# Tokens side by side as weights in the variance's small products, and the factor written to DRAM in single numbers

## Chip, cores and metric

One core of a Trainium2 chip runs the kernel. The metric is the device time of one execution in microseconds (us). Engines are named as in the profile: PE (TensorE's matmuls), PEld (its weight loads), DVE (VectorE), ACT (ScalarE), POOL (GpSimd), SP (SyncE, here the issuer of nearly all DMAs).

## What is computed

Linear attention over 8 batches of 576 tokens with 8 heads of 64 features, then two feed-forward layers. The change lies in the normalisation at the head of the first of these:

```python
rms = np.sqrt(np.mean(x * x, axis=-1, keepdims=True) + 1e-06)
xn = x / rms * rms_g
g = xn @ w_gate
silu = g * (1.0 / (1.0 + np.exp(-g)))
val = xn @ w_val
return (silu * val @ w_out)
```

Here `x` has 4608 tokens of 512 features, and `w_gate` and `w_val` have 1536 columns each. `1 / rms` is one number for each token; it is called the factor below. The second layer takes the maximum of three products and multiplies it by an output matrix.

## The kernel before

The 4608 tokens are worked in nine groups of 512 (`NG`, `N`). Activations lie by feature: a tile has 128 features on its partitions and 512 tokens along its free dimension, and four such tiles make one group's x. The first mixture layer is a loop over groups g and over 12 slices f of the hidden features, `iteration(g, nxt, f)`; each iteration runs 24 products of 128x128 weights with 128x512 tokens (`product_in`, L601 to L603) into two PSUM banks, `pg` and `pv`. Each product is made from three with operands split into a high and a low part. While group g is multiplied, the attention of the group after next and the normalisation of the next one, `nxt`, are worked out in between, at fixed iterations; products of the second mixture's weights (class `Ahead`) are prepared beside them.

The steps that make the factor of group `nxt` are these, for `nxt` from 3 to 8:

- `make_x` squares the attention's output (ACT) and adds the four tiles of squares up (POOL, L518), so that `sacc[nxt]` holds for each of 128 partitions and 512 tokens a partial sum of squares.
- `token_rstd` (at f = 7) sums over the partitions. Four products on L551 take 128 tokens of `sacc` each as weights and a column of ones as the moving operand; each puts one column with 128 sums into `pv`. The trace shows each of these products as two loads and two matmuls, so that a group has eight. `pv` has 128 partitions and 4 columns.
- DVE turns these into the factor by three Newton steps (L552 to L559), in `z`, of 128 partitions by 4 numbers.
- `z` is put on the list `later`. At the start of the next iteration SP writes it to `rstd_dram[nxt]` in DRAM, 512 numbers in the order of the tokens.
- `read_rstd` (at f = 9) reads these 512 numbers back, the same row for all 128 partitions, into `rooms["zb"]`.
- `normalise` (at f = 10, DVE, L583) multiplies the four tiles of x by it, and `split_x` (at f = 11) makes high and low parts, which the first product of the next group reads.

The factor has to lie in DRAM token by token. Groups that are not in `COMPACT` (groups 3 to 8) choose the tokens so that each partition holds neighbours: column t of the product takes tokens t, t + 4, t + 8 and so on, so that partition r ends with tokens 4r to 4r + 3. Groups 0 to 2 don't go by DRAM; groups 1 and 2 take tokens side by side (128t to 128t + 127) and spread the factor by transposes (`spread_rstd`).

Every DMA of SP is issued by the helper `sp` (L143 from group 1 on, L145 ahead of that), in the order in which the program has them. SP takes them one after the other, and a DMA that waits holds up those behind it. The DMAs take turns on eight semaphores, and each waits until the last one on its own semaphore has landed. The statistics of q (`stats_dram`) go through DRAM in the same way as the factor: `put_stat` writes them, `spread_stats` reads them, in four DMAs of which each fills 64 partitions of one of two planes.

Here are SP's rows from the write of group 3's factor on, with what each waits for. `rstd` is the factor's place in DRAM, `stats` that of q's statistics, `rooms_o` rooms for tiles that are used again, `w_dram` the prepared weights, `h_dram` the stored hidden features, `kT` and `q` inputs of the attention.

```order
L143 DMA rstd_194<-z_3_2702 128x4 [waits DMAHW0_49,DVE_49]
L143 DMA h_dram_2_116<-h_7_2742 128x512 [waits DMAHW1_49,DVE_49]
L143 DMA w_dram_146<-rooms_o_1420 128x512 [waits DMAHW2_49,Pool_49]
L143 DMA w_dram_158<-rooms_o_1421 128x512 [waits DMAHW3_49,Pool_49]
L143 DMA w_dram_155<-rooms_o_1420 128x512 [waits DMAHW4_49,Pool_49]
L143 DMA stats_1_172<-qr_1_2689 128x2x4 [waits DMAHW5_49]
L143 DMA rooms_o_1422<-in_qt 128x512 [waits DMAHW6_49]
L143 DMA kT_2_2776<-in_kt 128x576 [waits DMAHW7_49]
L143 DMA q_3_2778<-in_q 128x512 [waits DMAHW0_49,Activation_49]
```

The last of them, q, is the eighth behind the write and waits for the write's own semaphore, `DMAHW0`.

Of the kernel before, what the change touches and what calls it, by code (L numbers as in the profile page):

```python
# [25 lines left out]
COMPACT = (0, 1, 2)  # L26
# [29 lines left out]
def attention_moe_moe(ctx: ExitStack, tc: tile.TileContext, q, qt, k, kt, v, w1, w1_out, rms_g, w2, w2_out, out):  # L56
# [23 lines left out]
    def bank(tag, name):  # L80
        return ps.tile([P, N], F32, tag=tag, name=name)
# [34 lines left out]
    rstd_dram = [dram.tile([N], F32, tag=f"rstd_{g}", name=f"rstd_{g}") for g in range(NG)]  # L116
# [12 lines left out]
    for i in range(2):  # L129
        t = one.tile([P, P], F32, tag=f"kv_raw{i}", name=f"kv_raw{i}")  # L130
# [17 lines left out]
    later, rooms = [], {}  # L148
# [158 lines left out]
    kmax, xraw, sacc, qrt, rstd = {}, {}, {}, {}, {}  # L307
# [229 lines left out]
    def token_rstd(g):  # L537

        var = one.tile([P, LINE], F32, tag="var0", name=f"var0_{g}")[:, 0:4]
        if g == 0:  # L540
            for t in range(4):
                nc.vector.tensor_scalar(
                    var[:, t : t + 1], sacc[0][t][:, 0:1], 1.0 / N, EPS_RMS, op0=ALU.mult, op1=ALU.add
                )
        else:
            pv = bank("a1" if g < BY_FEATURE else "acc2", f"pv_{g}")
            for t in range(4):
                s = sacc[g][:, t * P : (t + 1) * P]
                if g not in COMPACT:
                    s = sacc[g].rearrange("p (r t) -> p t r", t=4)[:, t, :]  # L550
                nc.tensor.matmul(pv[:, t : t + 1], s, ones_f[:, 0:1], start=True, stop=True)  # L551
            nc.vector.tensor_scalar(var, pv[:, 0:4], 1.0 / N, EPS_RMS, op0=ALU.mult, op1=ALU.add)  # L552
        z = one.tile([P, LINE // 2], F32, tag="z0", name=f"z0_{g}")[:, 0:4]
        nc.vector.tensor_scalar(z.bitcast(I32), var.bitcast(I32), -0.5, RSQRT_SEED, op0=ALU.mult, op1=ALU.add)
        a = one.tile([P, LINE // 2], F32, tag="a0", name=f"a0_{g}")[:, 0:4]
        for i in range(3):
            nc.vector.scalar_tensor_tensor(a, z, 0.25**i, z, op0=ALU.mult, op1=ALU.mult)
            nc.vector.tensor_mul(a, a, var)
            nc.vector.scalar_tensor_tensor(z, a, -3.0, z, op0=ALU.add, op1=ALU.mult)  # L559
        rstd[g] = z  # L560
        if g == 0:
            spread_rstd(g)
        if g not in COMPACT:
            later.append((rstd_dram[g].rearrange("(r t) -> r t", t=4), z))

    def read_rstd(g):
        sp(rooms["zb"], rstd_dram[g].unsqueeze(0).to_broadcast([P, N]))
# [2 lines left out]
    def spread_rstd(g):  # L570
        z = rstd[g]
        pr = bank("a1", f"rstd_{g}")
        for t in range(4):
            nc.tensor.transpose(pr[:, t * P : (t + 1) * P], z[:, t : t + 1].to_broadcast([P, P]), ident)
        if g < BY_FEATURE:
            zb = one.tile([P, N], F32, tag="ql", name=f"z_{g}")
        else:
            zb = rooms["zb"]
        nc.scalar.copy(zb, pr)
        rstd[g] = None, zb  # L580
# [43 lines left out]
    for step in range(11):  # L624
        for stage, t in stages:
            if 0 <= step - t < 4:
                stage(0, step - t)
    token_rstd(0)
    for stage in (first.scale, first.join, first.high, first.low):
        for h in range(2):  # L630
# [217 lines left out]
    def iteration(g, nxt, f):  # L848
# [18 lines left out]
        if nxt == 1:  # L867
            if not odd and 1 <= pair <= 4:
                transpose_q(nxt, pair - 1)
                make_kv(nxt, pair - 1)  # L870
                if pair + 1 < 4:
                    load_pair(nxt, pair + 1)
            if odd and 1 <= pair <= 4:
                make_x(nxt, pair - 1)
            if pair < 4 and not odd:
                k_max(nxt, pair)
                q_exp(nxt, pair)
            if pair < 4 and odd:
                k_exp(nxt, pair)
                q_divide(nxt, pair)  # L880
            if f == 10:
                token_rstd(nxt)
            if f == 11:
                for p in range(4):
                    normalise(nxt, p)
# [44 lines left out]
        if nxt is not None and nxt >= BY_FEATURE:  # L930
            if f == at:
                token_rstd(nxt)
            if f == at + 2 and nxt not in COMPACT:
                read_rstd(nxt)
            if f == 10 and nxt > BY_FEATURE:
                for p in range(4):
                    normalise(nxt, p)
# [256 lines left out]
    for pr in range(NPAIR):  # L1194
        behind = []
        for u in range(UNITS):
            fp, j = divmod(u, 3)
            if j == 0:
                t = {
                    key: two.tile([P, N], F32, tag=tag, name=f"t2_{pr}_{fp}_{tag}")  # L1200
                    for key, tag in (((0, 0), "q"), ((0, 1), "k"), ((1, 0), "v"))
                }
# [21 lines left out]
    g = NG - 1  # L1224
# [28 lines left out]
    for u in range(UNITS):  # L1253
        fp, j = divmod(u, 3)
        pair = [bank(tag, f"p2_{g}_{u}_{tag}") for tag in (("G", "V"), ("a0", "a1"))[u % 2]]
        if j == 0:
            t = [two.tile([P, N], F32, tag=tag, name=f"t2_{g}_{fp}_{tag}") for tag in ("q", "k")]
# [83 lines left out]
```

## Time and profile before

| | us |
|---|---|
| median of 3 runs | 1511.15 |
| lowest, highest | 1510.17, 1512.53 |
| the profiled execution, its own time | 1514.36 |
| its span, first to last instruction | 1512.2 |

The profiled execution's time has 2.2 us around its span. The rows further below are from this execution; a time of day in them counts from the span's start. "Idle before" in brackets behind a row is how long the engine stood before it, and behind the arrow stands what ended that.

### The profile page before, as it was taken

How to read it: one execution, taken by the hardware profiler on the slowest of the kernel's cores; microseconds unless marked ns; L12 is line 12 of the kernel's file. 1: busy time of each engine (PE TensorE's matmuls, PEld its weight loads, DVE VectorE, ACT ScalarE, POOL GpSimd, SP SyncE). 2: the span in 40 equal slices, each digit the busy share in tenths (PEclk: the TensorE clock that was granted, in tenths of full speed). 3: DMA queues.
4: the chain of work that ended last, by engine and by line, in shares of the span. 5: the costliest groups of instructions: out<-in, count | busy, mean ns of one | idle time of the engine just before them, and what ended most of it. 6: DMA issues, size and time to landing. Idle time of an engine off the chain costs nothing.

```text
span 1512.2 us, 19762 instructions
## 1 busy us (share of the span) xinstructions
PE 1479.8 (98%) x6692; PEld 1220.0 (81%) x6692; DVE 1059.5 (70%) x1769; ACT 611.0 (40%) x1176; POOL 446.6 (30%) x380
## 2 busy tenths in 40 slices
PE   6899999999999999999999999999999999999999
PEld 4677878788878888888888888888888888888887
DVE  6998786778676765472888989748748748747622
ACT  7754443435343444341545545323423413413311
POOL 0012544444344344351265764111111111111100
PEclk9999999999999999999999999999999999999999
DMA  8866988878887967588545245265585585585572
GB/s 263 307 197 175 258 248 244 268 215 259 245 259 217 265 187 262 195 285 318 177 170 195 82 162 202 79 226 197 194 296 194 194 305 190 189 288 190 181 261 102
DMA packets 159333, 330.30 MB, mean 218 GB/s; under 512 B 31104, under 2 KB 55680, under 8 KB 159232
## 3 DMA queue, kind: packets, MB, share of 16 engines
q1 hardware_dynamic: 155776, 322.74, 65.8%
q10 hardware_dynamic: 3456, 6.29, 1.1%
q8 instruction: 53, 0.87, 0.2%
q14 instruction: 48, 0.39, 0.1%
HBM read 246.42 MB, written 82.55 MB: 218 GB/s over the span
## 4 chain that ended last, share of the span: by engine, by line
PE 70%; DVE 6%; DMA 3%; issue 2%; ACT 1%; SPq 1%; POOL 1%; DVEq 0%; POOLq 0%
PE p_a L608 4%; PE p_a L607 4%; PE p_a L609 4%; PE pg L602 4%; PE pg L601 4%; PE pg L603 4%; PE pv L603 4%; PE pv L602 4%; PE pv L601 4%; PE o_acc L608 3%; PE o_acc L609 3%; PE o_acc L607 3%; PE p_G L607 2%; PE p_G L608 2%; PE p_G L609 2%; PE o_a L607 2%
## 5 line engine op out<-in xcount | busy, mean ns | idle before, releaser
L1067 POOL TENSOR_TENSOR temps_wl<-temps_wl,temps_wh 128x512 f32<-128x512 f32 x36 | 48.2, 1340 | 348.4 <-ACT temps_wh L1066 273.8
L273 POOL TENSOR_TENSOR rooms_o<-st,rooms_o 128x256 fp32r<-128x256 f32 x77 | 65.0, 852 | 126.3 <-ACT rooms_o L272 119.7
L960 DVE SCALAR_TENSOR_TENSOR t<-t,pg 128x512 f32<-128x512 f32 x64 | 43.9, 686 | 69.2 <-ACT t L959 68.5
L1058 DVE TENSOR_TENSOR temps_wl<-temps_wl,p_a 128x512 f32<-128x512 f32 x72 | 49.2, 683 | 37.3 <-POOL temps_wl L1067 37.1
L419 POOL TENSOR_TENSOR q<-q,qm 128x512 f32<-128x512 f32 x29 | 31.8, 1097 | 144.7 <-DVE ks L457 97.7
L1062 ACT COPY temps_wh<-p_G 128x512 f32<-128x512 f32 x36 | 21.1, 587 | 105.9 <-PE p_G L609 105.5
L973 DVE SCALAR_TENSOR_TENSOR h<-t,pv 128x512 f32<-128x512 f32 x66 | 45.2, 685 | 26.3 <-PE pv L603 23.5
L607 PE MATMUL p_a<-x_wh,chunk 128*128 128x512 f32 x160 | 62.2, 389 | 0.0
L608 PE MATMUL p_a<-x_wh,chunk 128*128 128x512 f32 x160 | 62.2, 389 | 0.0
L609 PE MATMUL p_a<-x_wh,chunk 128*128 128x512 f32 x160 | 62.2, 389 | 0.0
L607 PE MATMUL p_a<-x_wl,chunk 128*128 128x512 f32 x160 | 62.2, 389 | 0.0
L608 PE MATMUL p_a<-x_wl,chunk 128*128 128x512 f32 x160 | 62.2, 389 | 0.0
L609 PE MATMUL p_a<-x_wl,chunk 128*128 128x512 f32 x160 | 62.2, 389 | 0.0
L959 ACT ACTIVATE t<-pg 128x512 f32<-128x512 f32 x64 | 37.8, 591 | 51.2 <-PE pg L603 48.8
L1064 DVE TENSOR_TENSOR temps_wl<-temps_wh,p_V 128x512 f32<-128x512 f32 x36 | 24.6, 684 | 43.9 <-PE p_V L609 43.9
L762 POOL TENSOR_TENSOR h_Z<-h_Z,h_X 128x512 f32<-128x512 f32 x24 | 39.8, 1678 | 44.8 <-DVE h_X L755 41.0
L758 POOL TENSOR_TENSOR h_X<-h_Y,h_X 128x512 f32<-128x512 f32 x24 | 40.4, 1694 | 38.9 <-DVE o_xl L101 21.6
L960 DVE SCALAR_TENSOR_TENSOR rooms_o<-rooms_o,pg 128x512 f32<-128x512 f32 x42 | 28.6, 682 | 31.3 <-ACT rooms_o L959 31.1
L272 ACT CAST rooms_o<-st 128x256 fp32r<-128x256 f32 x77 | 31.8, 423 | 39.8 <-DMA w_dram<-rooms_o 16.1
L453 PEld LDWEIGHTS pk<-v,k 128*128 128x128 f32 x300 | 40.5, 204 | 6.4 <-ACT k L444 3.9
L453 PE MATMUL pk<-v,k 128*128 128x129 f32 x300 | 42.2, 290 | 2.9 <-ACT k L444 2.3
L959 ACT ACTIVATE rooms_o<-pg 128x512 f32<-128x512 f32 x42 | 24.9, 593 | 45.3 <-PE pg L603 45.1
(1232 smaller groups left out, 4978.7 us busy)
## 6 DMA issues: line engine op xcount, KB each, us to landing
chunk<-w_dram SPq DMA_DIRECT2D x112, 768.0 KB, 4.3
w_dram<-rooms_o SPq DMA_DIRECT2D x113, 256.0 KB, 3.4
h_dram<-h SPq DMA_DIRECT2D x108, 256.0 KB, 4.4
stat<-stats SPq DMA_DIRECT2D x112, 128.0 KB, 5.3
words<-in_w SPq DMA_DIRECT2D x24, 512.0 KB, 6.6
chunk<-w_dram SPq DMA_DIRECT2D x48, 256.0 KB, 3.6
k<-in_k SPq DMA_DIRECT2D x30, 320.0 KB, 4.6
v<-in_v SPq DMA_DIRECT2D x30, 320.0 KB, 6.1
```

What stands on the lines that cost most here:

```text
L273: nc.gpsimd.tensor_sub(t[:, 1, :], src, t[:, 0, :].bitcast(F32))
L453: nc.tensor.matmul(pk[:, 0 : P + 1], k_t[g, p][:, c, :], v_t[g, p][:, c, :], start=(c == 0), stop=(c == 4))
L601: nc.tensor.matmul(pt, hi[:, j, s], xhs[kk], start=(kk == 0), stop=False)
L602: nc.tensor.matmul(pt, hi[:, j, s], xls[kk], start=False, stop=False)
L603: nc.tensor.matmul(pt, lo[:, j, s], xhs[kk], start=False, stop=(kk == 3))
L607: nc.tensor.matmul(pt, ah, bh, start=first, stop=False, skip_group_check=onto)
L608: nc.tensor.matmul(pt, ah, bl, start=False, stop=False, skip_group_check=onto)
L609: nc.tensor.matmul(pt, al, bh, start=False, stop=last, skip_group_check=onto)
L959: nc.scalar.activation(t, pg, AF.Tanh, scale=0.5)
L960: nc.vector.scalar_tensor_tensor(t, t, 1.0, pg, op0=ALU.add, op1=ALU.mult)
L1058: nc.vector.tensor_add(y, x, pt)
L1067: nc.gpsimd.tensor_add(w, u2, s5)
```

## The change

Two lines of `token_rstd`: the products of all groups take 128 tokens that lie side by side, as groups 1 and 2 do, and column t then holds tokens 128t to 128t + 127. The write to DRAM puts number t of partition r at place 128t + r instead of 4r + t. What lies in DRAM after it, and the read of it, are as before.

```diff
             for t in range(4):
                 s = sacc[g][:, t * P : (t + 1) * P]
-                if g not in COMPACT:
-                    s = sacc[g].rearrange("p (r t) -> p t r", t=4)[:, t, :]
                 nc.tensor.matmul(pv[:, t : t + 1], s, ones_f[:, 0:1], start=True, stop=True)
...
         if g not in COMPACT:
-            later.append((rstd_dram[g].rearrange("(r t) -> r t", t=4), z))
+            later.append((rstd_dram[g].rearrange("(t r) -> r t", t=4), z))
```

No instruction is added, taken away or moved on any engine, and no wait changes. On SP six rows have another form; this is the piece for group 3, with the row ahead of the write and the one behind it:

```order
 L143 DMA stat_0_2679<-stats_0_171 64x512 [waits DMAHW7_49]
-L143 DMA rstd_194<-z_3_2702 128x4 [waits DMAHW0_49,DVE_49]
+L143 DMA rstd_194<-z_3_2702 128x4x1 [waits DMAHW0_49,DVE_49]
 L143 DMA h_dram_2_116<-h_7_2742 128x512 [waits DMAHW1_49,DVE_49]
 L143 DMA w_dram_146<-rooms_o_1420 128x512 [waits DMAHW2_49,Pool_49]
```

The write goes out as 128 x 4 pieces of one number each where it was 128 pieces of four numbers.

## Rows read from the trace of the kernel before

**Rows 1.** Page, part 1: busy us (share of the span) xinstructions.
```profile
PE 1479.8 (98%) x6692; PEld 1220.0 (81%) x6692; DVE 1059.5 (70%) x1769; ACT 611.0 (40%) x1176; POOL 446.6 (30%) x380
```

**Rows 2.** Busy time by stretch: us, PE, PEld, DVE, ACT, POOL, granted clock, DMA share, GB/s.
```profile
195.00:720.00 525.00, 520.34 (x2406) 433.43 (x2405) 340.37 (x653) 213.26 (x420) 218.99 (x211) 1.00 0.81 247
```

**Rows 3.** Weight loads of L551, 195 to 700 and 100 to 195 us: ns min/median/max.
```profile
L551 PEld LDWEIGHTS pv<-ones_f,sacc x48: 308/329/332, 245.9 to 628.6; 128*128 128x128 f32 x48
...
L551 PEld LDWEIGHTS pv<-ones_f,sacc x16: 187/192/192, 107.4 to 182.5; 128*128 128x128 f32 x16
```

**Rows 4.** PE's timeline at group 2's and group 3's burst: start us, us.
```profile
181.80 0.95 PE L551 MATMUL pv<-ones_f,sacc 128*128 128x1 f32 x8
182.61 0.48 PE L601 MATMUL pg<-x,wh_(1, 9)_1184 128*128 128x512 f32 x1
...
245.99 1.92 PE L551 MATMUL pv<-ones_f,sacc 128*128 128x1 f32 x8
247.78 0.47 PE L601 MATMUL pg<-xh,wh_(1, 7)_1041 128*128 128x512 f32 x1
```

**Rows 5.** Chain of waits, the bursts that it holds: start us, us.
```profile
323.25 1.76 PE pv L551 x8
...
477.18 1.76 PE pv L551 x8
...
552.97 1.64 PE pv L551 x8
...
627.38 1.64 PE pv L551 x8
```

**Rows 6.** Chain of waits ahead of group 5's stage, three of its pieces.
```profile
386.74 0.70 DVE h L973
...
403.32 5.11 DMA stat<-stats
...
421.77 5.80 DMA rooms_o<-rstd
```

**Rows 7.** PE's timeline where it stood idle; in brackets the idle time before.
```profile
116.35 0.62 PE L574 MATMUL rstd<-ident,z 128*128 128x128 f32 x4 [2.21 <-DVE z L559]
...
279.87 0.50 PE L601 MATMUL pg<-x,wh_(1, 0)_506 128*128 128x512 f32 x1 [0.18 <-ACT x L100]
281.63 0.50 PE L602 MATMUL pg<-x,wh_(1, 0)_506 128*128 128x512 f32 x1 [1.25 <-DVE x L101]
...
432.58 2.36 PE L453 MATMUL pk<-v,k 128*128 128x129 f32 x10 [1.79 <-ACT k L444]
```

**Rows 8.** Timelines of DVE, SP and POOL behind group 3's burst.
```profile
246.08 0.69 DVE L973 SCALAR_TENSOR_TENSOR h<-t,pv 128x512 f32<-128x512 f32 x1 [0.45 <-PE pv L603]
...
249.33 2.87 SPq L143 DMA_DIRECT2D stat<-stats  x4
...
257.65 1.29 POOL L380 TENSOR_TENSOR qT<-qT,stat 128x512 f32<-128x512 f32 x1 [1.70 <-DMA stat<-stats]
```

**Rows 9.** Busy time by stretch around two idle times; the clock stands third from the end.
```profile
114.00:117.00 3.00, 0.79 (x6) 0.68 (x6) 2.83 (x10) 1.05 (x2) 0.52 (x1) 1.00 0.00 0
...
432.00:437.00 5.00, 4.42 (x17) 3.99 (x18) 5.00 (x10) 2.64 (x5) 1.33 (x1) 0.66 0.95 294
```

**Rows 10.** DMA queue from 631 to 633 us, group 8's write alone: packets, MB, share.
```profile
q1 hardware_dynamic: 144, 0.00, 3.8%
```

**Rows 11.** DMA issues of the whole span, the factor's write: KB, median us to landing.
```profile
rstd<-z SPq DMA_DIRECT2D x6, 2.0 KB, 4.9
```

**Rows 12.** SP's timeline: a load in 640 pieces, then group 4's write and read.
```profile
248.68 0.59 SPq L143 DMA_DIRECT2D v<-in_v  x1
...
335.13 0.38 SPq L143 DMA_DIRECT2D rstd<-z  x1
...
345.98 0.33 SPq L143 DMA_DIRECT2D rooms_o<-rstd  x1
```

**Rows 13.** SP's waits from 485 to 496 us: total us, times, longest.
```profile
SPq L143 <- DMA rstd<-z: 0.6, 1, 0.6
```

## The prediction

> **What bounds the kernel now.** I read the page's busy times first, then the busy time by stretch, then the small products by themselves, the chain of waits, and last what DVE, SP and POOL do where TensorE (PE below) waits. The page gives PE 98% of the span [rows 1]; in the stage of the first mixture, 195 to 720 us, which holds all six places that the change touches, PE is busy for 520.34 of 525 us at the full clock [rows 2]. So an instruction that gets shorter on PE here is worth its time, unless the chain of waits passes that place by on other engines. That exception decides this case.
>
> "The burst of group g" is the run of variance products on L551 for group g: four products, recorded as eight loads and eight matmuls. It stands in the stage of the group before. All groups' loads have the same 128 columns. The 16 of groups 1 and 2, whose weights are tokens side by side, take 192 ns in the median; the 48 of groups 3 to 8, whose weights are every fourth token, take 329 ns [rows 3].
>
> **The change, part by part.**
>
> *The six bursts.* After the change they read what group 2 reads today. From the burst's start to the next product's start, group 2 needs 182.61 - 181.80 = 0.81 us, group 3 needs 247.78 - 245.99 = 1.79 us [rows 4]; both have a transpose right ahead of them. The saving is 0.98 us. The chain gives the bursts of groups 4 and 6 1.76 us each, those of groups 7 and 8 1.64 us each [rows 5]; so I count 0.98 for groups 3 to 6 and 0.98 - 0.12 = 0.86 for groups 7 and 8. Together 4 x 0.98 + 2 x 0.86 = 5.64 us of PE time.
>
> *What of it lies on the path.* The chain runs through four of the bursts, those of groups 4, 6, 7 and 8 [rows 5]. It doesn't run through the other two.
> - Group 5: at 386.74 the chain has left PE for DVE, goes on through SP's issues, a read of the q statistics at 403.32 and the read of the factor at 421.77, and comes back to PE only at 432.58, where PE had stood idle for 1.79 us [rows 6, 7]. The burst at 398 lies beside that. A faster PE only waits longer there: 0.
> - Group 3: the chain as traced starts later than this, so I followed it by hand. The burst starts at 245.99 [rows 4]. DVE makes h at 246.08 from a product that stands ahead of the burst; SP issues four reads of statistics at 249.33; POOL stands idle for 1.70 us for one of them and subtracts at 257.65 [rows 8]. From there it goes by ACT, POOL and SP, with no product behind the burst in it that ends last, to the two idle times of PE at 279.87 and 281.63, 0.18 and 1.25 us [rows 7]. So the 0.98 us turns into idle time there too: 0.
>
> What is left is 2 x 0.98 + 2 x 0.86 = 3.68 us. For groups 3 and 5 the bounds are 0 and the whole 0.98 each; I take 0, since PE already waits there for 1.43 and 1.79 us.
>
> *The factor's write.* Six times, 128 pieces of 16 bytes become 512 pieces of 4 bytes. The trace has no 4-byte piece. The nearest row is the write for group 8, alone on the queues: 144 packets take 3.8% of sixteen engines' 2 us, 0.076 us an engine, or 8.4 ns for each of its nine packets [rows 10]. At that price 384 more pieces, 24 an engine, cost 0.20 us. SP's issue of the write takes 0.38 us; a load of 640 pieces takes 0.59 [rows 12]; so at most 0.2 us more. That is 0.4 us a group.
>
> Its cover: the write lands 4.9 us after issue in the median [rows 11], and the shortest distance from write to read among the six is group 4's, 345.98 - 335.13 = 10.85 us [rows 12], which leaves 5.95 us. But each DMA on SP waits for the one eight places ahead, and in one group, 6, SP stood for 0.6 us waiting for this write [rows 13]. What is queued behind it there are loads of the next pairs and the stores of h. I charge the 0.4 us once, in that group. The bounds are 0 and 6 x 0.4 = 2.4 us.
>
> *The rest.* The order of instructions and their waits is the same on every engine, DVE's work on the factor has the same shape, and the read of the factor stays a read of one row for all partitions: 0.
>
> *Sum.* -3.68 + 0.4 = -3.28, say -3.3 us: 1514.36 - 3.3 = 1511.1 us for the profiled execution. That one stands 3.2 us above the median of the three runs; from the median it is 1511.15 - 3.3 = **1507.9 us**. A measurement can tell some 0.2%, 3.0 us, from no change, so this forecast lies barely beyond that.
>
> **The rivals.**
>
> *The clock falls once more (1509.5 us).* At 432.58 PE had been idle for 1.79 us, and the granted clock from 432 to 437 is 0.66 in the mean, part of it the lower level [rows 7, 9]: 5 x 0.34 = 1.7 us lost. Group 3's two idle times at 279.87 and 281.63 make 1.43 us today at the full clock; with 0.98 added they make 2.41 within some 3 us. For it: that is more than 1.79. Against it: at 116.35 an idle time of 2.21 us left the clock full [rows 7, 9]. So it can go either way. Price: 3.3 - 1.7 = 1.6 us gained.
>
> *All of it arrives (1505.9 us).* If the statistics' reads come earlier in other executions than in the profiled one, PE leads the path in groups 3 and 5 too, and 5.64 - 0.4 = 5.2 us come through; without the idle time at 432.58 the fallen clock's 1.7 us would go as well, 1504.2. Against it: gaps of 1.43 and 1.79 us have to close first.
>
> *Little of it arrives (about 1510.5 us).* Either the step between tokens is not what makes the loads long, or PE, once ahead, meets the normalised x at the start of groups 4, 6 and 8, which hang on the factor's read and not on PE. Against the first: same line, same columns, 192 against 329 ns [rows 3]. Against the second: the chain runs through these bursts, so what PE waits for later started behind them. I allow 0.7 us of gain.
> The Trainium skill, "TensorE: Matmul & The Clock Gate", section "LDWEIGHTS (loading the stationary operand)", makes a load's time depend on its columns alone. By that rule the two kinds of load would cost the same and the sum would be no gain, 1511.6 us with the write's 0.4; the rows above differ from it by 137 ns a load, so I follow the rows.
>
> *The write is too slow (about 1526 us).* This is the other side. If a 4-byte piece costs far more than the row's 8.4 ns, the factor comes late, DVE normalises late, and PE waits at the start of each group. Group 4's spare 5.95 us are gone at 5.95 / 24 = 0.25 us a piece, some thirty times the row; it decides from about 0.29 us, where six groups lose about 1 us each and the gain of 3.3 us turns into a loss beyond 3.0. At 0.5 us a piece the write lands 12 us later, group 4's read is 6 us late, and at half of that in the mean over six groups 18 us are lost: 1511.15 + 18 - 3.3 = 1525.9. Against it: at 16 bytes no packet came near such a price.
> The Trainium skill, "DMA: Bandwidth & Descriptors", sections "Specifications" and "Rules for kernel authors", speaks against this change: pieces under 512 bytes are written by read-modify-write, and a last dimension that isn't contiguous gives one descriptor per element and should be rearranged. It states no price for a 4-byte piece, and today's 16-byte pieces lie under its bound already; no run here shows one of 4 bytes.
>
> **How the numbers follow.** Forecast 0.42, its own range 1506.6 to 1509.2 (the write's cost between 0 and 2.4, and a little of groups 3 and 5), of which 0.26 lies below 1508.1. Clock 0.22, inside 0.2%. All arrives 0.16, faster. Little arrives 0.11, inside 0.2%. Slow write 0.09, slower. Faster 0.26 + 0.16 = 0.42; same 0.16 + 0.22 + 0.11 = 0.49; slower 0.09. The range from 1505.3 to 1510.6 holds the forecast, the clock, most of "all arrives" and most of "little arrives", some 0.82; it leaves out the slow write and the case of 1504.2.
>
> **What would show it.** Right: all 64 loads on L551 near 190 ns and six bursts of about 0.81 us; PE's idle time at the start of group 3's stage (281 us now) and ahead of the pk products at the start of group 5's (432 us now) about 1 us longer each; the write's landing within 1 us of today's; SP's row of waits for the factor's write not above a few tenths each. Wrong: loads still above 300 ns; a granted clock at the lower level near 280 us (the clock case); DVE waiting at the normalising products for the factor's read longer than today, or the write landing 10 us after its issue (the slow write); PE's waits in groups 3 and 5 unchanged with a shorter span (all arrives).

## The result, and the profile after the change

| | before | after |
|---|---|---|
| median of 6 runs each, us | 1511.68 | 1531.11 |
| lowest, highest | 1510.17, 1515.37 | 1527.84, 1534.52 |
| profiled execution, its time | 1514.36 | 1533.93 |
| its span, mean granted clock | 1512.2, 0.999 | 1531.8, 0.992 |

The ratio is 1.011, its 95% interval 1.0088 to 1.0131: the kernel became about 1.1% slower, some 17 us (the medians differ by 19.4), where 3.3 us of gain were forecast and 1510.6 us was the upper end of the range. In the changed kernel, lines of `token_rstd` and behind stand two lines higher: the burst is L549, the products L599 to L601, the normalising product L581.

First what came as forecast, the bursts. The first fence has the small products' weight loads (ns min/median/max), the second PE's timeline at group 3's burst (start us, us), both of the kernel after.

```profile
L549 PEld LDWEIGHTS pv<-ones_f,sacc x64: 187/192/192, 109.1 to 648.3; 128*128 128x128 f32 x64
```
```profile
246.44 0.95 PE L549 MATMUL pv<-ones_f,sacc 128*128 128x1 f32 x8
247.26 0.48 PE L599 MATMUL pg<-xh,wh_(1, 7)_1041 128*128 128x512 f32 x1
```

All 64 loads now take the 192 ns that only groups 1 and 2 had [rows 3], and the burst of group 3 takes 247.26 - 246.44 = 0.82 us where it took 1.79 [rows 4].

The page shows where to look for the loss: the span is 19.6 us longer, PE's busy time only 5.4 us longer than before [rows 1]. The second fence is the busy time by stretch, over the stage and over three pieces behind group 3's write (us, PE, PEld, DVE, ACT, POOL, granted clock, DMA share, GB/s).

```profile
span 1531.8 us, 19762 instructions
...
PE 1485.2 (97%) x6692; PEld 1221.5 (80%) x6692; DVE 1055.3 (69%) x1769; ACT 610.7 (40%) x1176; POOL 446.2 (29%) x380
```
```profile
195.00:740.00 545.00, 525.31 (x2414) 434.34 (x2413) 338.09 (x654) 213.58 (x421) 218.66 (x211) 0.98 0.84 238
...
255.00:257.00 2.00, 2.00 (x11) 1.62 (x10) 0.91 (x5) 0.73 (x2) 1.14 (x2) 1.00 1.27 263
257.00:262.00 5.00, 5.00 (x24) 4.10 (x23) 1.92 (x2) 1.21 (x3) 1.75 (x2) 1.00 1.31 65
262.00:264.00 2.00, 2.00 (x10) 1.65 (x10) 0.57 (x1) 0.62 (x1) 0.74 (x1) 1.00 0.77 94
```

In the stage, which now lasts until 740 us, PE stands idle for 545.00 - 525.31 = 19.7 us; before it was 525.00 - 520.34 = 4.7 [rows 2]. That is 15.0 us. The mean clock gives the next part: 0.008 x 1531.8 = 12.3 us below full speed, before 0.001 x 1512.2 = 1.5, so 10.7 us. Less the 5.6 us that the bursts gave, the sum is 20.1 us, beside the 19.6 by which the span grew (the mean clocks are rounded to 0.001, so either product can be off by 0.8).

The pieces from 255 on say what made PE wait. Group 3's write is issued at 253.94. From 257 to 262 the DMA share is 1.31, and 65 GB/s are moved (the recorded times of packets overlap, so a share can lie above 1). The same stretch of the kernel before:

```profile
257.00:262.00 5.00, 5.00 (x24) 4.09 (x23) 1.15 (x3) 2.09 (x5) 2.59 (x2) 1.00 0.95 223
```

So the transfers issued around the write crawl. Next, the issue groups of the kernel after (KB each, median us from issue to landing): the write over the whole span, then the stretch from 650.7 to 652 us, where group 8's write stands alone, with the queue's row (packets, MB, share of sixteen engines) ahead of it.

```profile
rstd<-z SPq DMA_DIRECT2D x6, 2.0 KB, 10.7
```
```profile
q1 hardware_dynamic: 535, 0.02, 22.2%
...
rstd<-z SPq DMA_DIRECT2D x1, 2.0 KB, 10.7
```

The kernel before, at the issue of group 8's write:

```profile
rstd<-z SPq DMA_DIRECT2D x1, 2.0 KB, 1.4
```

The median landing went from 4.9 us [rows 11] to 10.7; for the kernel after the trace has a landing for three of the six writes only, those of groups 6 to 8. For group 8 it went from 1.4 us to 10.7. Its packets show next to none of that: with some others they are through within 1.3 us, at 22.2% of it, 0.29 us an engine. The write then takes 9 us more to count as landed, and for the first 2.9 of them, until SP issues the next store at 654.93, no data moves on the queue at all.

How it reaches PE is told by the chain of waits, here for groups 3 and 5 (start us, us), and by PE's, ACT's and POOL's timelines.

```profile
250.36 6.02 DMA stat<-stats
256.44 11.57 DMA w_dram<-rooms_o
...
268.51 0.65 ACT k L444
269.20 2.52 PE pk L453 x10
...
412.12 11.07 DMA stat<-stats
...
423.35 1.29 POOL qT L382
...
428.69 0.75 ACT k L444
```
```profile
268.09 0.42 ACT L272 CAST rooms_o<-rooms_o 128x256 fp32r<-128x256 f32 x1 [1.26 <-DMA w_dram<-rooms_o]
268.42 0.73 ACT L444 ACTIVATE k<-k 128x640 f32<-128x640 f32 x1
```
```profile
423.35 1.28 POOL L382 TENSOR_TENSOR qT<-qT,stat 128x512 f32<-128x512 f32 x1 [5.71 <-DMA stat<-stats]
```
```profile
269.20 2.52 PE L453 MATMUL pk<-v,k 128*128 128x129 f32 x10 [4.03 <-ACT k L444]
...
429.48 2.52 PE L453 MATMUL pk<-v,k 128*128 128x129 f32 x10 [5.10 <-ACT k L444]
...
509.91 2.41 PE L453 MATMUL pk<-v,k 128*128 128x129 f32 x10 [2.83 <-ACT k L444]
...
527.80 0.50 PE L599 MATMUL pg<-xh,wh_(1, 0)_506 128*128 128x512 f32 x1 [2.04 <-ACT xh L100]
```

In group 3's place a store of prepared weights (`w_dram`), the third of three issued behind the write, takes 11.57 us. The three in the median, the kernel before first:

```profile
w_dram<-rooms_o SPq DMA_DIRECT2D x3, 256.0 KB, 4.6
```
```profile
w_dram<-rooms_o SPq DMA_DIRECT2D x3, 256.0 KB, 10.5
```

ACT's cast of the next weights waits for its room, ACT's exponential of k on L444 stands behind that cast on the same engine, and PE waits 4.03 us for it. In group 5's place a read of q's statistics lasts from 412.12 for 11.07 us, where it took 5.11 [rows 6]; POOL waits 5.71 us for it, and PE 5.10 us at the end of that chain. This read was issued ahead of the write, as SP's timeline shows, so a transfer need not queue behind the write to suffer from it:

```profile
410.17 2.55 SPq L143 DMA_DIRECT2D stat<-stats  x4
412.82 0.53 SPq L143 DMA_DIRECT2D rstd<-z  x1
```

PE's waits in the stage, the kernel after, and behind them the first of these in the kernel before (us in total, times, longest):

```profile
PE pk L453 <- ACT k L444: 13.3, 5, 5.1
PE pg L600 <- DVE xl L101: 2.3, 2, 1.3
PE pg L599 <- ACT xh L100: 2.2, 2, 2.0
```
```profile
PE pk L453 <- ACT k L444: 2.3, 2, 1.8
```

SP, too, stood for the write itself, in five waits, where before it was one of 0.6 us [rows 13]:

```profile
SPq L143 <- DMA rstd<-z: 4.9, 5, 2.7
```

Behind the long idle times of PE the clock falls. Busy time by stretch, the columns as above, the clock in the third column from the right:

```profile
269.00:275.00 6.00, 5.80 (x20) 5.06 (x21) 5.25 (x12) 2.55 (x6) 1.99 (x3) 0.54 0.96 298
429.00:435.00 6.00, 5.52 (x18) 4.87 (x19) 2.50 (x7) 2.31 (x6) 3.19 (x4) 0.50 0.86 222
509.00:515.00 6.00, 5.09 (x20) 4.56 (x21) 3.89 (x10) 2.42 (x6) 1.22 (x2) 0.72 0.92 237
```

0.50 is the lower of the clock's two levels (1.2 of 2.4 GHz) for the whole of six microseconds. In these three pieces alone 6 x (0.46 + 0.50 + 0.28) = 7.4 us of the full clock are missing.

### The profile page after: what moved, and what is told of

Its sections match the earlier page's. It is cut to its first block, busy times and chain, and to the rows that moved or that the text cites. A ratio compares the mean times of both kernels' runs of the same rounds, so it can differ in the third digit from the quotient of the medians.

```text
span 1531.8 us, 19762 instructions
## 1 busy us (share of the span) xinstructions
PE 1485.2 (97%) x6692; PEld 1221.5 (80%) x6692; DVE 1055.3 (69%) x1769; ACT 610.7 (40%) x1176; POOL 446.2 (29%) x380
## 4 chain that ended last, share of the span: by engine, by line
PE 66%; DMA 8%; DVE 7%; issue 2%; SPq 2%; ACT 1%; POOL 1%; DVEq 0%; POOLq 0%; ACTq 0%
PE p_a L606 4%; PE p_a L605 4%; PE p_a L607 4%; PE o_acc L606 3%; PE o_acc L605 3%; PE o_acc L607 3%; PE pg L600 3%; PE pv L601 3%; PE pv L600 3%; PE pg L601 3%; PE pv L599 3%; PE pg L599 3%; PE p_G L605 2%; PE p_G L606 2%; PE p_G L607 2%
## 5 line engine op out<-in xcount | busy, mean ns | idle before, releaser
L758 POOL TENSOR_TENSOR h_Y<-h_W,h_Y 128x512 f32<-128x512 f32 x24 | 38.1, 1599 | 10.5 <-DMA h_W<-h_dram 10.0
```

## The experiments

The theory was: the six writes of 512 single numbers cost all of the loss, and they do it by slowing the transfers near them, not by a late factor. Against it stood, in turn: that the shorter bursts themselves start the reads at a worse time; that the queue or semaphores of SP are held up; that it is the number of pieces, whatever their place; that it is the order of the places, or that neighbours come from different partitions. Letters in the expectations stand for this theory (A, with numbers for ideas of what makes the write slow) and for its rivals. Ratios are to runs of the kernel before on the same chip.

### The two halves of the change apart, and the write on another queue

e1_loads keeps the new weights and writes as before, 128 pieces of 16 bytes:

```diff
-            later.append((rstd_dram[g].rearrange("(t r) -> r t", t=4), z))
+            later.append((rstd_dram[g].rearrange("(r t) -> r t", t=4), z))
```

> The changed kernel's loads (tokens side by side) with the old write, 128 pieces of 16 bytes in the old places; so the factor lies in DRAM in another order of tokens, and the output is another. Theory A, the write's 512 pieces cost all of the loss: 1508 us (1506 to 1510.5), the write lands after some 5 us as before. Rival B, the shorter bursts themselves upset PE's rhythm (PE ahead, idle, clock falling): 1520 us or more.

Measured: 1510.73 us beside 1513.82, ratio 0.9983 (0.9969 to 0.9996). The write lands after 4.7 us in the median, group 8's after 1.4. So the bursts by themselves gain some 2.6 us (0.6 to 4.7 by the interval); the 3.68 us that the prediction put on the path lie inside that.

e2_write keeps the old weights and writes as the changed kernel does, that is, in the kernel before:

```diff
-            later.append((rstd_dram[g].rearrange("(r t) -> r t", t=4), z))
+            later.append((rstd_dram[g].rearrange("(t r) -> r t", t=4), z))
```

> The old loads (every fourth token) with the changed write, 512 pieces of 4 bytes; the factor lies in DRAM in another order of tokens. Theory A: slower than the changed kernel by what the bursts save, 1533 us (1529 to 1538), the write lands after 10 to 12 us. Rival B: 1511 to 1515 us.

Measured: 1534.65 us beside 1513.82, 1.0148 (1.0124 to 1.0173). The whole loss is the write's, about 22 us for six. The issue row of e2_write:

```profile
rstd<-z SPq DMA_DIRECT2D x6, 2.0 KB, 11.0
```

e6_act is the changed kernel with the six writes issued by ACT, so that they don't stand in SP's queue:

```diff
-            sp(dst, src)
+            if src is rstd.get(nxt):
+                nc.scalar.dma_start(dst, src)
+            else:
+                sp(dst, src)
```

> The changed kernel with the factor's write issued by ACT's queue instead of SP's; same pieces, same places, and it doesn't count among SP's eight semaphores. Theory A: the write holds up the DMA engines and the memory themselves, so other transfers crawl as before: 1525 us or more, DMA rate below 110 GB/s for 5 us behind it. Rival C, what costs is SP's queue (the semaphore eight places on and the order within SP's rings): 1508 to 1514 us.

Measured: 1535.52 us beside 1512.48, 1.0139 (1.0115 to 1.0163). The write, and the stretch from 257 to 262 us, in e6_act:

```profile
rstd<-z ACTq DMA_DIRECT2D x6, 2.0 KB, 10.7
```
```profile
257.00:262.00 5.00, 5.00 (x24) 4.05 (x24) 1.81 (x3) 1.94 (x4) 1.60 (x2) 1.00 1.24 109
```

The landing is the same from another queue, and the other transfers move at 109 GB/s where the kernel before moves 223. So neither the slow landing nor the slow neighbours come from the write's place in SP's queue. The time of this run can't say what SP's waits cost, though. The expectation takes the write as free of SP's eight semaphores, and the trace shows that it is not: SP stands for it longer than in the changed kernel (4.9 us).

```profile
SPq L143 <- DMA rstd<-z: 30.5, 6, 10.3
```

Against SP's waits as the main cause in the changed kernel speak their 4.9 us in all beside 15.0 us more of idle time on PE, and the chains of groups 3 and 5, in which a store and a read that each took over 11 us come last. How much of the loss goes by SP's waits is not separated by these runs.

### How many pieces, or how close together

e3_pairs writes 256 pieces of two numbers, one beside the other with no space between:

```diff
-            later.append((rstd_dram[g].rearrange("(t r) -> r t", t=4), z))
+            later.append((rstd_dram[g].rearrange("(a r b) -> r a b", a=2, b=2), z.rearrange("p (a b) -> p a b", a=2)))
```

> The changed kernel with the write in 256 pieces of 8 bytes (two numbers of a partition side by side); the factor lies in DRAM in another order. Theory A1, each piece costs the whole DMA system some 15 ns, one behind the other (5.8 us more for 384 more pieces): landing near 6.8 us, and a third of the loss, 1508 + 23 x 128/384 = 1516 us (1511 to 1520). Rival A2, only pieces below 8 bytes are dear: landing near 5 us and 1508 us.

Measured: 1515.56 us, 1.0018 (1.0006 to 1.003), and the write lands after 6.7 us in the median. That is what a price for each piece (A1) foretold, 1516 us and 6.8; the next runs show that the agreement was luck.

e5b_near and e5_far write 512 single numbers again, but each to a place of its own 64 or 512 bytes from the next, in a spare array; the factor that is read was written once, early.

```diff
+    rstd_all = dram.tile([N], F32, tag="rstd_all", name="rstd_all")
+    rstd_dram = [rstd_all] * NG
+    far_dram = [dram.tile([N, 16], F32, tag=f"far_{g}", name=f"far_{g}") for g in range(NG)]
...
+            sp(rstd_all.rearrange("(r t) -> r t", t=4), z)
...
-            later.append((rstd_dram[g].rearrange("(t r) -> r t", t=4), z))
+            later.append((far_dram[g][:, 0].rearrange("(t r) -> r t", t=4), z))
```

(e5_far has 128 where this has 16.)

> As the run in which the pieces went to a spare array, but in the changed kernel's order (number t of partition r to place 128t + r) and 64 bytes from one number to the next; the factor's array is written once, early, so the factors are wrong. Theory A3, numbers of different engines beside each other in DRAM hold each other up: group 8's write, alone on the queues, lands in some 3.6 us or less, the median near 8 us, the time 1518 to 1524 us. Rival A4, the order t-major itself is dear (each partition's four numbers far apart): group 8's write lands near 10.7 us and the time is 1527 us or more.

> The same with 512 bytes from one number to the next. Theory A3: as at 64 bytes, 3.6 us or less for group 8's write alone. Rival A5, the distance that has to be kept is larger than 64 bytes: 64 bytes land near 10.7 us and 512 bytes near 3.6. Rival A4: both near 10.7 us.

Measured: 1513.71 and 1512.98 us beside 1512.48, 0.9997 (0.9979 to 1.0016) and 0.9996 (0.998 to 1.0011). The issue rows, e5b_near first, then e5_far:

```profile
far<-z SPq DMA_DIRECT2D x6, 2.0 KB, 4.9
```
```profile
far<-z SPq DMA_DIRECT2D x6, 2.0 KB, 5.4
```

Group 8's write alone, in e5b_near:

```profile
far<-z SPq DMA_DIRECT2D x1, 2.0 KB, 1.8
```

The same 512 pieces of four bytes land about as fast as the 128 pieces of 16 bytes did, and the median and the time are below the 8 us and the 1518 to 1524 us that A3 gave; A4 and A5 are out. So the number of pieces is not what costs, and neither is their size alone. What is left is how close together they lie.

e11_half, e13_quarter and e10_mixed8 are e5b_near with 8, 4 and 2 numbers to a place (32, 16 and 8 bytes apart). e4_local is e10_mixed8 with the pieces in the order of the old write, so that neighbours come from one partition:

```diff
-            later.append((far_dram[g][:, 0].rearrange("(t r) -> r t", t=4), z))
+            later.append((far_dram[g][:, 0].rearrange("(r t) -> r t", t=4), z))
```

> The same with 32 bytes from one number to the next, 2 to each 64 bytes. If sharing 64 bytes is what costs, a little more than at 64 bytes apart (1.8 us alone): 2 to 3 us for group 8's write, ratio 0.999 to 1.002. If the unit is 32 bytes or less: as at 64 bytes apart, 1.8 us.

> 512 pieces of 4 bytes to the spare array in the changed kernel's order with 16 bytes from one to the next, 4 to each 64 bytes; factors wrong as in the other runs with the spare array. Between 8 bytes apart (3.1 us alone) and 32 (1.9 us): 2 to 2.6 us, ratio 0.998 to 1.002. If it stays at 1.9 us, 4 pieces to 64 bytes cost nothing, and the dear ones begin at 8.

> 512 pieces of 4 bytes to the spare array in the changed kernel's order with 8 bytes from one to the next, so 8 numbers to 64 bytes, from several partitions; factors wrong as in the other runs with the spare array. Theory A6, only the number of pieces in the same 64 bytes counts: as with the partition's own order at 8 bytes, group 8's write alone lands in some 3.6 us, ratio 1.005. Rival A3, it matters that neighbours come from different partitions and engines: well above 3.6 us, 6 us or more, ratio 1.006 to 1.010.

> The changed kernel with 512 pieces of 4 bytes as before the run, but number t of partition r goes to place 4r + t of a spare array at 8 bytes from one to the next, so that neighbours in DRAM come from one partition and one DMA engine; the factor's array itself is written once, early, so the factors are wrong. Theory A1, the count of pieces decides: landing 10 to 11 us, 1526 to 1536 us as the changed kernel. Rival A3, neighbours in DRAM written by different engines get in each other's way: landing below 7 us and 1507 to 1512 us.

e12_dense_own writes 512 single numbers with no space between them, also in the old order. It is e1_loads with the factor's four numbers in every second column of `z`, so that they can't go out as one piece:

```diff
-        z = one.tile([P, LINE // 2], F32, tag="z0", name=f"z0_{g}")[:, 0:4]
+        z = one.tile([P, LINE // 2], F32, tag="z0", name=f"z0_{g}")[:, 0:8].rearrange("p (t two) -> p t two", two=2)[:, :, 0]
```

> Side-by-side loads; the factor's write again in 512 pieces of 4 bytes without gaps in DRAM, but in the partition's own order (number t of partition r at 4r + t), which the source's gaps keep from being joined to 16 bytes; the factors lie in another order of tokens. Each 64 bytes are then written by four neighbouring partitions, where the changed kernel has sixteen. Theory A6, the number of pieces in the same 64 bytes decides whoever writes them: group 8's write alone lands in some 10.7 us, ratio 1.011 or more. Rival A3, it matters that 64 bytes are written by many partitions and so by more than one engine: some 3 to 5 us alone, ratio 1.001 to 1.005.

All of them together, by how many pieces lie in the same 64 bytes (landings in us, the median of those in the trace, which are all six but for the last two rows with three each, and group 8's):

| run | pieces | in 64 bytes | landing | group 8's | ratio (95%) |
|---|---|---|---|---|---|
| e1_loads | 128 of 16 bytes | 4 | 4.7 | 1.4 | 0.9983 (0.9969 to 0.9996) |
| e5_far | 512 of 4 bytes, 512 bytes apart | 1 | 5.4 | 1.9 | 0.9996 (0.998 to 1.0011) |
| e5b_near | 512 of 4 bytes | 1 | 4.9 | 1.8 | 0.9997 (0.9979 to 1.0016) |
| e11_half | 512 of 4 bytes | 2 | 4.8 | 1.9 | 0.9992 (0.9976 to 1.0007) |
| e13_quarter | 512 of 4 bytes | 4 | 5.5 | 3.1 | 0.9985 (0.9971 to 0.9998) |
| e10_mixed8 | 512 of 4 bytes | 8 | 7.4 | 3.1 | 1.0022 (1.001 to 1.0034) |
| e4_local | 512 of 4 bytes, old order | 8 | 8.2 | 3.6 | 1.0053 (1.0034 to 1.0071) |
| e3_pairs | 256 of 8 bytes | 8 | 6.7 | 3.2 | 1.0018 (1.0006 to 1.003) |
| after | 512 of 4 bytes | 16 | 10.7 | 10.7 | 1.011 (1.0088 to 1.0131) |
| e12_dense_own | 512 of 4 bytes, old order | 16 | 11.7 | 8.1 | 1.0156 (1.0134 to 1.0178) |

Up to four pieces in 64 bytes the write costs no time that these runs can tell, though at four it lands later; at eight it costs some, at sixteen most. The number of pieces by itself doesn't decide: e3_pairs and e10_mixed8 have the same 8 bytes from piece to piece, 256 and 512 of them, and land and lose alike. The order doesn't decide either. Group 8's write of e12_dense_own, in which a partition's four numbers are neighbours, lands far above the 3 to 5 us of A3 (though below the 10.7 of A6), and the run loses at least as much as the changed kernel:

```profile
rstd<-z SPq DMA_DIRECT2D x1, 2.0 KB, 8.1
```

The theory that neighbours from different partitions, and so from different engines, are what hurts is not borne out: pieces in the partition's own order are no cheaper, in e12_dense_own or in e4_local, which met neither of its expectations. That 64 bytes are the unit is not shown. They are a way of counting: the runs change the step from number to number, and with it the length of the stretch that is written. At 32 bytes apart (e11_half) the write lands as at 64, which its expectation put down to a unit of 32 bytes or less, and e13_quarter at 16 bytes came out above its 2 to 2.6 us. In e4_local nothing reads what is written, and it still loses 0.5%: the loss needs no late factor. What makes crowded pieces slow, and why so much more at sixteen than at eight, no run shows. In these spare-array runs the factor's read no longer waits for the write, so their ratios, unlike their landings, also leave out that wait; a dense write that nothing reads was not tried.

### Other ways to have the tokens in order

e8_spread takes the factor off DRAM altogether: groups 3 to 8 spread it as groups 0 to 2 do, with transposes that stand between the products.

```diff
-            later.append((rstd_dram[g].rearrange("(t r) -> r t", t=4), z))
+            pass
...
-            if f == at + 2 and nxt not in COMPACT:
-                read_rstd(nxt)
...
+        if nxt is not None and nxt not in COMPACT and f == at + 1:
+            spread_rstd(nxt)
```

> Side-by-side loads; the factor of groups 3 to 8 doesn't go by DRAM but is spread over the partitions as in groups 1 and 2, by four transposes on PE (0.62 us a group) and an ACT copy (0.57 us), placed between the two products of the eighth iteration; the output is the reference's. Theory A: no write, no read; PE gives back 0.62 of the 0.98 us, and the DVE wait for the read in group 5 goes: 1507 to 1511 us, no slower than before. Rival: the transposes wait for the factor on PE: 1512 to 1516 us.

Measured: 1514.26 us beside 1512.48, 1.0005 (0.9992 to 1.0018), above theory A's range. No slow write, and no gain either: each group's four transposes now stand on PE, with 0.60 us in each of groups 3 to 5, so some 3.6 us for the six. PE waits for k six times where e1_loads had one such wait, but no longer in total. PE's waits in e8_spread, 195 to 740 us, and behind them that of e1_loads:

```profile
PE pk L453 <- ACT k L444: 3.2, 6, 1.1
PE pv L599 <- DVE h L971: 1.2, 1, 1.2
```
```profile
PE pk L453 <- ACT k L444: 3.3, 1, 3.3
```

e9_view keeps the new weights and the old write, and lets DVE take the order right when it reads the factor, every fourth number of it:

```diff
-            later.append((rstd_dram[g].rearrange("(t r) -> r t", t=4), z))
+            later.append((rstd_dram[g].rearrange("(r t) -> r t", t=4), z))
...
-        nc.vector.tensor_mul(xraw[g, p], xraw[g, p], rstd[g][1])
...
+        x = xraw[g, p].rearrange("p (t r) -> p t r", t=4)
+        nc.vector.tensor_mul(x, x, rstd[g][1].rearrange("p (r t) -> p t r", t=4))
```

> Side-by-side loads, the old write of 128 pieces of 16 bytes and the old read; the order is put right on DVE: the four normalising products read the factor with a step of four numbers (a view of the tile in SBUF), so no piece of DRAM is smaller than before. Output as the reference. Theory A: the bursts' saving without the write's cost, 0.997 to 0.9995 of the kernel before, as in the run with the loads alone. Rival D, a step of 16 bytes is dear on DVE as it was on the weight loads: the products take 1.0 us or more in place of 0.69, and the time is that of the kernel before or up to 0.3% above it.

Measured: 1518.1 us beside 1514.33, 1.0024 (1.0012 to 1.0037). The normalising products by line, e9_view first, then e1_loads (ns min/median/max):

```profile
L585 DVE TENSOR_TENSOR xraw<-xraw,rooms_o x24: 1025/1078/1649, 277.5 to 653.3; 128x512 f32<-128x512 f32 x24
```
```profile
L581 DVE TENSOR_TENSOR xraw<-xraw,rooms_o x28: 640/684/1783, 195.1 to 645.9; 128x512 f32<-128x512 f32 x28
```

A step of 16 bytes in one operand makes a product 1078 ns long where it is 684. Four stand in a row ahead of each group's first product, 4 x 0.39 = 1.6 us a group, PE's waits for x on L604 come to 4.9 us where e1_loads had 1.3 on L600, and the gain is gone, as rival D had it.

e7_rows turns the factor before it is written. One transpose makes of `z`, 128 partitions by 4, a tile of 4 partitions by 128; DVE copies it out of PSUM, and SP writes four pieces of 512 bytes. It stands one iteration behind `token_rstd`, between the products.

```diff
-        if g not in COMPACT:
-            later.append((rstd_dram[g].rearrange("(t r) -> r t", t=4), z))
+
+    def put_rstd(g):
+        pr = bank("a1", f"rstd_{g}")
+        nc.tensor.transpose(pr[0:4, 0:P], rstd[g], ident)
+        row = one.tile([P, P], F32, tag="rrow", name=f"rrow_{g}")[0:4, :]
+        nc.vector.tensor_copy(row, pr[0:4, 0:P])
+        sp(rstd_dram[g].rearrange("(t r) -> t r", t=4), row)
...
+        if nxt is not None and nxt not in COMPACT and f == at + 1:
+            put_rstd(nxt)
```

> Side-by-side loads; PE transposes the factor once (4 rows of 128 numbers in PSUM), DVE copies it, and SP writes 4 pieces of 512 bytes an iteration's half later than before; the read stays in its place. Output as the reference. Theory A: nothing is held up by the write, and a transpose of 4 columns costs PE about 0.3 us of the 0.98 saved: 0.9975 to 1.000 of the kernel before. Rival E, the write is now so near the read that SP waits for it: DVE waits for the read by 2 us or more in most groups, 1.001 to 1.006.

Measured: 1508.46 us beside 1514.33, 0.9969 (0.9955 to 0.9984), just below theory A's range. Its output is the reference's, and it beats both kernels. The stage, the added copies, and PE's waits, in e7_rows:

```profile
195.00:720.00 525.00, 521.71 (x2445) 432.59 (x2444) 345.77 (x664) 215.76 (x424) 219.11 (x211) 1.00 0.81 249
```
```profile
L566 DVE COPY rrow<-rstd x6: 279/279/280, 258.2 to 630.5; 4x128 f32<-4x128 f32 x6
```
```profile
PE pk L453 <- ACT k L444: 1.3, 1, 1.3
...
PE pb L442 <- DVE rrow L566: 0.4, 1, 0.4
```

PE is idle for 3.3 us of the stage, less than before, its clock stays full, and the six copies cost DVE 0.28 us each.

## Why the prediction was wrong

**The bursts were right.** 192 ns a load, 0.82 us for the burst, as the rows of groups 1 and 2 foretold [rows 3, 4]. Alone (e1_loads) they gave 2.6 us, where 3.68 were put on the path and 5.64 were the whole. PE's wait for k grew to 3.3 us in that run, from 2.3, which fits what was said of groups 3 and 5: what a faster PE gains where other engines lead is idle time.

**The step that failed is "*The factor's write*".** Its term was 0.4 us, charged once, with 2.4 us as the upper bound. The six writes cost 19 to 26 us: 1.3% from the changed kernel against e1_loads, 1.5% in e2_write, 1.7% from e12_dense_own against e1_loads. The price of a piece was not what was off. The packets took 0.29 us an engine with some others among them, and 0.076 + 0.20 was foretold. What was wrong is taking the packets' time for the write's price. "Its cover" then asked only whether the landing would pass the read, by 5.95 us, and what is queued on SP's semaphores. It didn't ask what a write in flight does to the transfers around it, and that is where the loss comes from in the two places that were followed to PE, groups 3 and 5.

**The nearest row was too far.** It was a piece of 16 bytes, four in 64 bytes; e13_quarter has four-byte pieces at that same density and loses nothing (0.9985), though it lands later (3.1 us alone). Sixteen in 64 bytes were outside what the trace of before shows, and the upper bound was drawn from the same row as the value. The one row that could have warned was the landing itself, 1.4 us for the write alone: its packets take 0.076 us of that.

**The rival of the slow write had the side and nearly the size, by another way.** It gave 1526 us against 1531.11, and the sign that it named, a landing some 10 us after the issue, is there. But its mechanism is not: DVE does not wait longer for the factor. These are its waits in the tile's view, the kernel after first, then the kernel before (us, times):

```profile
  DVE xraw L581: 2.9, 5
```
```profile
  DVE xraw L583: 5.6, 5
```

The loss comes by the statistics' reads and the stores of weights, in the places that were followed. So it is luck that 1526 lies near the result. Its "decides from about 0.29 us" a piece was tied to the factor's path, and doesn't hold. A chance of 0.09 was too low for a piece that no row showed.

**The rule of the Trainium skill that was set aside spoke for that side.** The Trainium skill, "DMA: Bandwidth & Descriptors", sections "Specifications" and "Rules for kernel authors", says that pieces under 512 bytes are written by read-modify-write, and that a last dimension which isn't contiguous should be rearranged. The result agrees in direction, and e7_rows, which writes pieces of 512 bytes, has the lowest ratio here, though its interval overlaps that of e1_loads. No run shows how a short piece is written. The size alone is not the price, though: e5b_near's four-byte pieces, far below that bound too, land alone in 1.8 us, against 10.7 for the crowded ones.

**The clock rival was right that idle time costs clock, but not about place or size.** It was priced at one fall of 1.7 us near 280 us, behind some 2.4 us of idle time. Behind idle times of 4.03 and 5.10 us, at 269 and 429 us, the clock's mean over six microseconds was 0.54 and 0.50; in all it took some 10.7 us of the loss, by the rounded means above. "The rest" at 0 and "all of it arrives" don't matter beside this.

## What to carry to other kernels

Price a scattered write by its time to land and by what the transfers around it then move, not by the busy time of its packets; where the trace has no write of that kind, the upper bound is everything near it that waits for a DMA. Where a tiny result has to lie in DRAM in another order than on its partitions, turn it on the chip first, so that it goes out in a few long pieces. Look at every operand's step: weights and DVE operands read 16 bytes apart cost more than half again their time in these runs.

## What the runs showed of the hardware

- 512 pieces of four bytes are nearly free when they lie 32 or 64 bytes apart (they land alone in 1.9 and 1.8 us) and dear when they lie side by side (10.7 us in the changed kernel, 8.1 in e12_dense_own, 11.2 in e6_act). At 16 and 8 bytes apart they land alone in 3.1 to 3.6 us.
- A write can be in flight long after its last packet: group 8's 512 pieces end by about 652 us, and it lands at 650.77 + 10.7 = 661.5. Behind group 3's write the other transfers lose most of their rate (65 against 223 GB/s), while the DMA engines are shown as busy (a share of 1.31).
- A weight load of 128 columns of four-byte numbers takes 192 ns with tokens side by side and 329 with every fourth [rows 3]; a DVE product of 512 takes 684 ns, and 1078 with every fourth number of one operand.
